# Weight bits in a PSUM bank, four heads through one bank in single pieces, and a new order of the opening and the first 16 steps

## The chip, the cores and the metric

The kernel runs on one core of one Trainium2 chip. The metric is the device time of one execution in microseconds (us). Engine names are those of the profile: PE does matmuls and transposes (PEld its weight loads), DVE, ACT and POOL are the vector, scalar and GpSimd engines, SP issues the DMAs. PE runs at one of two clocks, 2.4 or 1.2 GHz; the profile gives the granted clock as a share of the full one.

## The reference

Three parts in a row, for 4 batches of 576 tokens with 8 heads of 64 (2304 tokens of 512):

```python
scores = scale * np.matmul(q, k.transpose(0, 1, 3, 2))          # attention
mask_plain = (rel >= 0) & (rel < window)                        # heads 0-3, window 32
mask_dil = (rel >= 0) & (rel < window * dilation) & (rel % dilation == 0)   # heads 4-7, dilation 4
attn = softmax(np.where(mask, scores, -1e9)); x = attn @ v
...
h = x @ w_in                                                    # first MoE stage, d_ff 2048
g = h * np.cos(h)
x = g @ w_out
...
logits = x @ w_gate + noise_scale * noise                       # 8 experts, the best two of each token
out = sum over its two experts of weight * (relu(x @ w1[e]) @ w2[e])
```

## The kernel before

**Tiles and steps.** The tokens lie in 9 blocks of 256. The first MoE stage has 8 weight pairs p; one step is one block with one weight pair. The list `steps` has pairs p = 0 to 7, each for blocks 0 and 1 (16 steps), and then blocks 2 to 8 one after the other. Attention is cut into 16 "heads" u, each two heads of one batch; blocks 0 and 1 need heads 0 to 3, and heads 4 to 7 are worked beside steps 0 to 15. So the first 16 steps are also the time in which all weights arrive: each pair comes as four pieces of 512 columns.

**A weight piece.** `w_load` (L270) loads 512 KB of 64-bit numbers. `w_bits` makes 32-bit floats of their bits in three DVE operations on 128x512 elements (L291, L292, L293); the result `cut` lies in SBUF, and so do both inputs of L292 and L293. `w_parts` splits `cut` in a high part on ACT (L299) and a low part on POOL (L300). 4 pieces are cut in the opening, 28 beside steps 0 to 15.

**A head.** Scores in two halves of 5 and 4 blocks (mask matmul L422, product L431), the row maximum on DVE (L444, L446), nine Exp on ACT (L461, with a table load if another function was last), norm (POOL L475), three groups of transposes (PE L486) with their eviction (L489 on ACT, L491 on DVE), two output halves `mo` (PE L506), and the copy of these to `xraw` (L514, L523; on ACT in the opening, on DVE for heads 4 to 7). `x_split` makes the two float parts of x (ACT L548, DVE or POOL L549).

**A step.** The loop runs g1 (24 matmuls, L563, into a bank `ph`); position -1; ACT L571 and DVE L572; the first half of g2 of the step two before (6 matmuls, L590); position 0; Sin and Square on ACT (L574, L575) and DVE L576; position 1; g on ACT and POOL (L579, L580); the second half of that g2; position 2. The table `BESIDE` says which pieces of weights and heads are issued at which step and position. The string `OPENING` does the same for the time ahead of step 0: Q and V load a head, W, B, P stand for `w_load`, `w_bits`, `w_parts`, S, E, N, T, A for scores, Exp, norm, transposes and output of a head, X for `x_split`, G for a chunk of g1; steps 0 and 1 have three of their four chunks there.

**What sets the order.** Each engine takes its instructions in the order of the program and waits for their inputs. SP issues all loads in that order too. PSUM has 8 banks: two named `mid` that transposes, scores and output halves of heads 4 to 7 take in turn, two `ph`, four `acc`.

Of the kernel before, what the change touches and what calls it, by code (L numbers as in the profile page):

```python
# [208 lines left out]
def kernel(ctx: ExitStack, tc: tile.TileContext, qT, kT, v, wm, we, wg, noise, out):  # L209
# [66 lines left out]

    CUT = {}
# [38 lines left out]
    warm = psum.tile([P, 512], F32, tag="mid", name="warm", bufs=2)  # L316
# [86 lines left out]
    SM = {}  # L403

    def a_scores(u):
# [5 lines left out]
        if u in (2, 3):  # L411
            o = 4096 - (u - 1) * NB * KW
            s = ahead[2][:, o:o + NB * KW].rearrange("p (i k) -> p i k", k=KW)
        else:
            s = apool.tile([P, NB, KW], F32, tag="s", name=f"s{u}", bufs=2)
        mx = small.tile([P, NB], F32, tag="mx", name=f"mx{u}", bufs=3)
        for g, (i0, i1) in enumerate(((0, 5), (5, NB))):
            n = i1 - i0
            sc = psum.tile([P, 512], F32, tag=tag, name=f"sc{u}_{g}", bufs=bufs)
# [31 lines left out]
        U[u][2] = s  # L451

    def a_exp(u):
        s = U[u][2]
        if u not in SC:
            nc.scalar.activation(s, s, AF.Exp, scale=0.125)
            return
        mx, *s3 = SC.pop(u)
        sm = small.tile([P, NB], F32, tag="sm", name=f"sm{u}", bufs=3)
        for i in range(NB):  # L460
            nc.scalar.activation(s[:, i, :], s3[i // 5][:, i % 5, :], AF.Exp, scale=0.125, bias=mx[:, i:i + 1],  # L461
                                 accum_out=sm[:, i:i + 1])
        SM[u] = sm

# [13 lines left out]
    def a_trans(u, c, scalar=True):  # L478
        s = U[u][2]
        if u < 4:  # L480
            at = ahat[:, 3 * (u % 3) + c]
        else:
            at = apool.tile([KW, 3, P], F32, tag="at", name=f"at{u}_{c}", bufs=2)
        mid = psum.tile([P, 512], F32, tag="mid", name=f"mt{u}_{c}", bufs=2)
        for j in range(3):
            nc.tensor.transpose(mid[:KW, j * P:(j + 1) * P], s[:, 3 * c + j, :], ident)  # L486
        m3 = mid[:KW, :3 * P].rearrange("p (j q) -> p j q", q=P)
        if scalar:
            nc.scalar.activation(at, m3, AF.Copy)  # L489
        else:  # L490
            nc.vector.tensor_copy(at, m3)  # L491
        U[u][3 + c] = at

    def a_av(u, g, scalar=False):
        b, hp = divmod(u, 4)
        half = S // 2
        tag, bufs = ("mid", 2) if u >= 4 else ("acc", 4)
        mid = psum.tile([P, 512], F32, tag=tag, name=f"mo{u}_{g}", bufs=bufs)
# [17 lines left out]
        else:  # L516
            m3 = mid[:, :half].rearrange("p (r j) -> p r j", r=2)
            done = 0
            while done < SJ:
# [4 lines left out]
                done += n  # L524

# [225 lines left out]
    for u in range(4, FUSED):  # L751
        at_step(START[u - 4] + 2, -1, a_norm, u)
        at_step(START[u - 4] + 3, 0 if u == 4 else -1, a_part, u, 0)
    pieces = [(0, 2), (0, 3)] + [(j, k) for j in range(1, NPAIR) for k in range(4) if (j, k) > (1, 1)]
    for n, (j, k) in enumerate(pieces):
        i = n // 2
        if n % 2:
            at_step(i, 2, w_bits, j, k)
            at_step(*((i, 2) if i - 1 in START else (i + 1, 0)), w_parts, j, k)
        else:  # L760
            at_step(i, 0, w_bits, j, k)
            at_step(i, 1, w_parts, j, k)
        if j == NPAIR - 1:
            at_step(i - 2, 2, w_piece, j, k)
    for u in range(4, 16):
        i = START[u - 4]
        if i > 0:
            at_step(i, 2, a_scores, u)
        if i > 0:
# [5 lines left out]
        at_step(i + 3, 2, a_part, u, 1)  # L775
        at_step(i + 4, 0, a_part, u, 2)
# [107 lines left out]
    def t_trans(e, t):  # L884
# [7 lines left out]
        mid = psum.tile([P, 512], F32, tag="mid", name=f"mgx{e}_{t}", bufs=2)  # L892
# [87 lines left out]

    known = {f.__name__ + "(" + ",".join(map(str, a)) + ")": (f, a) for fs in extras.values() for f, a in fs}
# [9 lines left out]
    for i, (blk, p) in enumerate(steps):  # L991
        if i == 48:
# [130 lines left out]
    with tc.If(over > CAP):  # L1123
        nt = nc.values_load(nti[0:1, 1:2], min_val=NTILE, max_val=NTILE + -(-(NT - CAP) // P))
        with tc.For_i(NTILE, nt, 1) as i:
            with tc.For_i(0, NE, 1) as e:
# [17 lines left out]
                mid = psum.tile([P, 512], F32, tag="mid", name="gm", bufs=2)  # L1144
# [62 lines left out]
```

## Time and profile before

| | |
|---|---|
| median of 3 runs | 1021.38 us (1019.44 to 1021.94) |
| the profiled execution | 1020.52 us, span 1018.8 us, mean granted clock 0.988 |
| PE busy over the span | 979.7 us, 96% |
| DVE, ACT, POOL busy | 551.1 (54%), 458.2 (45%), 358.4 us (35%) |

A busy engine runs an instruction; a matmul at the lower clock is busy for longer. The share over the whole span is a mean over stages. Up to about 40 us the opening runs, up to about 168 us the 16 steps beside which weights and heads 4 to 7 are worked, and after that the steps have all weights.

### The profile page before, as it was taken

What the parts mean: (1) busy time and instruction counts of PE and PEld (TensorE: products, weight loads), DVE (VectorE), ACT (ScalarE), POOL (GpSimd) and SP (SyncE); (2) the same over time, 40 slices, a digit from 0 to 9 for tenths busy, and PEclk for the clock granted to TensorE, in tenths of its full rate; (3) what the DMA queues carried; (4) which work ended last, traced back from release to release, by engine and by line L of the source; (5) the groups of instructions that cost most, each with busy time, mean ns of one, the idle gap of its engine ahead of it and who ended that gap; (6) DMA issues with size and microseconds to landing.
All of it is one profiled execution on the core that took longest, in us unless ns stands there. A gap on an engine that the chain in (4) does not pass through costs nothing.

```text
span 1018.8 us, 16807 instructions
## 1 busy us (share of the span) xinstructions
PE 979.7 (96%) x6560; PEld 864.1 (85%) x6560; DVE 551.1 (54%) x1149; ACT 458.2 (45%) x909; POOL 358.4 (35%) x470
## 2 busy tenths in 40 slices
PE   8788899999999899999999999999999999999996
PEld 6676778988898788898887889898898979898895
DVE  7799885357653755443556756344453535354321
ACT  6646665565655565454555434233241414232110
POOL 5555554233343442424243232231313232322302
PEclk9898999999999999999999999999999999999999
DMA  9963203134221220000052555453434244441201
GB/s 210 325 219 101 81 25 74 57 94 123 58 92 35 64 42 15 22 1 22 2 201 76 138 153 169 141 168 113 152 123 150 73 164 139 148 161 40 84 11 59
DMA packets 70594, 105.11 MB, mean 103 GB/s; under 512 B 31252, under 2 KB 44820, under 8 KB 70513
## 3 DMA queue, kind: packets, MB, share of 16 engines
q1 hardware_dynamic: 60528, 76.34, 24.8%
q0 software_dynamic: 9984, 27.68, 8.8%
q8 instruction: 52, 0.85, 0.4%
q14 instruction: 30, 0.24, 0.1%
HBM read 85.41 MB, written 19.59 MB: 103 GB/s over the span
## 4 chain that ended last, share of the span: by engine, by line
PE 69%; DVE 13%; ACT 6%; DMA 5%; issue 4%; POOL 1%; SPq 1%; ACTq 0%; POOLq 0%; DVEq 0%
PE ye L947 20%; PE pe L912 20%; PE ph L563 12%; PE acc L590 11%; DVE cut L292 3%; DMA raw<-in_wm 2%; PE mgx L895 2%; DVE r L572 1%; DVE cut L291 1%; PE sc L431 1%; DVE cut L293 1%; DVE r L576 1%; ACT r L574 1%; ACT r L575 1%; PE mo L506 1%
## 5 line engine op out<-in xcount | busy, mean ns | idle before, releaser
L563 PE MATMUL ph<-xhl,wm 128*128 128x256 f32 x1728 | 229.7, 289 | 10.4 <-ACT wm L299 4.3
L563 PEld LDWEIGHTS ph<-xhl,wm 128*128 128x128 f32 x1728 | 219.4, 195 | 18.4 <-ACT wm L299 4.7
L947 PE MATMUL ye<-we,h 128*128 128x512 f32 (+1 forms) x960 | 229.5, 395 | 0.0
L590 PE MATMUL acc<-wm,g 128*128 128x512 f32 x864 | 220.5, 399 | 3.1 <-POOL g L580 1.2
L947 PEld LDWEIGHTS ye<-we,h 128*128 128x128 f32 (+1 forms) x960 | 172.9, 183 | 42.9
L590 PEld LDWEIGHTS acc<-wm,g 128*128 128x128 f32 x864 | 156.9, 190 | 34.4 <-POOL g L580 2.1
L580 POOL TENSOR_TENSOR g<-r,g 128x512 fp32r<-128x512 f32 x72 | 95.7, 1330 | 206.9 <-ACT g L579 206.3
L912 PE MATMUL pe<-xga,we 128*128 128x352 f32 x768 | 125.5, 324 | 0.0
L912 PEld LDWEIGHTS pe<-xga,we 128*128 128x128 f32 x768 | 122.6, 188 | 0.4 <-issue 0.4
L960 POOL DMA_INDIRECT out<-old,tir x35 | 35.5, 1013 | 224.1 <-DVE old L958 219.3
L915 DVE SCALAR_TENSOR_TENSOR h<-pe,h 128x256 fp32r<-128x256 f32 (+1 forms) x128 | 60.5, 474 | 91.5 <-ACT h L914 86.0
L914 ACT ACTIVATE h<-pe 128x256 fp32r<-128x256 f32 (+1 forms) x128 | 54.3, 424 | 123.9 <-PE pe L912 112.6
L958 DVE SCALAR_TENSOR_TENSOR old<-ye,wts,old 128x512 f32<-128x512 f32 (+1 forms) x35 | 26.2, 750 | 135.6 <-PE ye L947 132.0
L912 PE MATMUL pe<-xgb,we 128*128 128x256 f32 x768 | 94.8, 284 | 1.5 <-DVE h L915 1.1
L912 PEld LDWEIGHTS pe<-xgb,we 128*128 128x128 f32 x768 | 93.3, 192 | 2.2 <-DVE h L915 1.3
L572 DVE SCALAR_TENSOR_TENSOR r<-r,ph 128x512 f32<-128x512 int32 x72 | 49.2, 683 | 82.2 <-ACT r L571 77.5
L576 DVE SCALAR_TENSOR_TENSOR r<-r,ph 128x512 f32<-128x512 f32 x72 | 49.4, 686 | 81.4 <-ACT r L575 81.3
L828 DVE TENSOR_TENSOR we<-wraw,we 128x512 fp32r<-128x512 f32 x128 | 88.9, 704 | 4.2 <-ACT g L579 0.9
L827 ACT ACTIVATE we<-wraw 128x512 fp32r<-128x512 f32 x128 | 78.0, 623 | 0.0
L574 ACT ACTIVATE r<-r 128x512 f32<-128x512 f32 x72 | 45.4, 631 | 63.8 <-DVE r L572 63.7
L571 ACT ACTIVATE r<-ph 128x512 int32<-128x512 f32 x72 | 42.6, 592 | 51.2 <-PE ph L563 51.0
L579 ACT ACTIVATE g<-r 128x512 fp32r<-128x512 f32 x72 | 45.4, 631 | 43.3 <-DVE r L576 27.7
(190 smaller groups left out, 1027.5 us busy)
## 6 DMA issues: line engine op xcount, KB each, us to landing
wraw<-in_we SPq DMA_DIRECT2D x64, 512.0 KB
raw<-in_wm SPq DMA_DIRECT2D x28, 512.0 KB
vts<-in_v SPq DMA_DIRECT2D x13, 384.0 KB
x1d<-x SPq DMA_DIRECT2D x9, 512.0 KB
out<-zt SPq DMA_DIRECT2D x18, 256.0 KB
kts<-in_kT SPq DMA_DIRECT2D x13, 288.0 KB
qts<-in_qT SPq DMA_DIRECT2D x26, 144.0 KB
piece<-in_wm SPq DMA_DIRECT2D x4, 512.0 KB
```

The source lines that it names most:

```text
L563: nc.tensor.matmul(ph[:, j, :], w[:, a, o:o + P], t[:, x, c, :], start=(c == 0 and n == 0 and (j == 0 or len(cs) == 4)), stop=(c == 3 and ...
L572: nc.vector.scalar_tensor_tensor(r, n, -TWO_PI, ph, op0=ALU.mult, op1=ALU.add)
L574: nc.scalar.activation(r, r, AF.Sin, scale=0.5)
L576: nc.vector.scalar_tensor_tensor(r, r, 0.5, ph, op0=ALU.subtract, op1=ALU.mult)
L580: nc.gpsimd.tensor_tensor(g[:, 1, :], r, g[:, 0, :].bitcast(F32), op=ALU.subtract)
L590: nc.tensor.matmul(ACC[blk][t], g[:, a, j * TB + t * P:j * TB + (t + 1) * P], w[:, x, 1024 + j * DM:1024 + (j + 1) * DM], start=(p == 0 an ...
L827: nc.scalar.activation(t[:, 0, fs], raw, AF.Copy)
L828: eng.tensor_tensor(t[:, 1, fs], raw, t[:, 0, fs].bitcast(F32), op=ALU.subtract)
L912: nc.tensor.matmul(ph[:, :n], w[:, a, o:o + P], x[:, b, c, :], start=(c == 0 and i == 0), stop=(c == 3 and i == 2))
L914: nc.scalar.activation(h[:, 0, f, :], ph[:, :n], AF.Relu)
L915: nc.vector.scalar_tensor_tensor(h[:, 1, f, :], ph[:, :n], 0.0, h[:, 0, f, :].bitcast(F32), op0=ALU.max, op1=ALU.subtract)
L947: nc.tensor.matmul(acc, h[:, a, f, o:o + n], w[:, b, (f % 4) * DM:(f % 4 + 1) * DM], start=(f == 0 and i == 0), stop=(f == 7 and i == 2))
```

## The change

**Bits.** In steps 0 to 15 (the list `alone` is not empty there) the first two DVE operations of `w_bits` write a PSUM bank (tag `cut`, one bank), and the third reads it and the raw piece and writes `cut` in SBUF. L309 and L310, as they are called now, have one input in SBUF instead of two. In the opening the bits stay in SBUF.

**Banks.** The bank comes from `mid`: there is one bank `mid` and one `cut` (`mid_tile`). In steps 0 to 15 all transposes, scores and outputs of heads 4 to 7 take the one bank `mid`; from step 16 on both are taken in turn as before.

**Pieces.** Heads 4 to 7 come in single pieces: `a_s` and `a_e` for half of the scores and of the Exp, `a_tr` for a third of the transposes, `a_o` for half of the output with its `xraw` copy on ACT (L546) and not on DVE. `w_parts` comes as `w_hi` (ACT, L319) and `w_lo` (POOL, L324). For heads 6 and 7 the Sin of a step stands between the two halves of Exp, so that ACT has four more table loads.

**Order.** `OPENING` and the rows of `BESIDE` for steps 0 to 15 are new.

```diff
 OPENING = (
-    "S0 S1 E0 N0 Q4 E1 W01 S2 W02 T00 T01 N1 E2 S3 T02 T10a N2 A00 T11 A01 W10 E3 W11 T12 T20a A10a T21a "
...
-    "B10 G10 W23 G11 W12 W21 E4 B11 A30a A31a X30 P10 P11 X31p G01 G02 G12 W13 W22"
+    "W01 S0 S1 E0 N0 E1 S2 N1 E2 T00 T01 S3 T10a E3 N2 W10 T11 T02 N3 A00 A10a A01 T20a T12 B00 T21a A11a "
+    "T30a Q4 W20 X01 X11p B01 A20a T32a T22a X00p X10 S4 P00 A21a W02 X21p G00 X20p V4 B10 G01 W13 G10 "
+    "G11 W03 P01 W11 E4 T31a A30a A31a W22 W12 W23 W21 B11 G12 X30 P10 P11 G02 X31p"
 )
 BESIDE = """
...
-4:1 w_parts(3,0) w_load(4,3) a_scores(5)
...
+4:1 a_loadv(5) w_hi(3,0) w_lo(3,0) a_s(5,0) w_bits(3,1) w_bits(3,2) a_e(5,0) w_hi(3,2)
+4:2 a_s(5,1) w_load(4,1)
...
+    def mid_tile(name):
+        turn[0] += not alone
+        return psum.tile([P, 512], F32, tag="mid" if alone or turn[0] % 2 else "cut", name=name, bufs=1)
...
-        V.tensor_scalar(t, hw, 3, 0x3FFFFFF8, op0=ALU.logical_shift_left, op1=ALU.bitwise_and)
-        V.scalar_tensor_tensor(t, hw, 0xC0000000, t, op0=ALU.bitwise_and, op1=ALU.bitwise_or)
-        V.scalar_tensor_tensor(t, lw, 29, t, op0=ALU.logical_shift_right, op1=ALU.bitwise_or)
+        b = psum.tile([P, 512], F32, tag="cut", name=f"bits{j}_{k}", bufs=1).bitcast(U32) if alone else t
+        V.tensor_scalar(b, hw, 3, 0x3FFFFFF8, op0=ALU.logical_shift_left, op1=ALU.bitwise_and)
+        V.scalar_tensor_tensor(b, hw, 0xC0000000, b, op0=ALU.bitwise_and, op1=ALU.bitwise_or)
+        V.scalar_tensor_tensor(t, lw, 29, b, op0=ALU.logical_shift_right, op1=ALU.bitwise_or)
...
-        tag, bufs = ("mid", 2) if u > 4 else ("ph", 2) if u == 2 else ("acc", 4)
...
+            if u > 4:
+                sc = mid_tile(f"sc{u}_{g}")
...
+    def a_o(u, g):
+        a_av(u, g, True)
...
+        if i == 0:
+            alone.append(True)
+        if i == 16:
+            alone.clear()
```

The order on ACT late in the opening, before (`mt3_1` and `mo3_0`, `mo3_1` are a transpose and the outputs of head 3, `sc4` the scores of head 4; the last row is the first operation of step 0):

```order
L299 ACTIVATE wm0_435<-cut0_1_466 128x512
L489 ACTIVATE ahat_89<-mt3_1_526 96x384
L461 ACTIVATE s4_504,sm4_559<-sc4_0_506,mx4_505 128x96 x5
L461 ACTIVATE s4_504,sm4_559<-sc4_1_516,mx4_505 128x96 x4
L523 COPY xraw_82<-mo3_0_573 128x2x144
L523 COPY xraw_82<-mo3_1_585 128x2x144
L548 ACTIVATE xhl0_448<-xraw_82 128x256
L299 ACTIVATE wm1_538<-cut1_0_539 128x512
L299 ACTIVATE wm1_538<-cut1_1_569 128x512
L548 ACTIVATE xhl1_445<-xraw_82 128x256
L571 ACTIVATE r0_0_633<-ph0_0_531 128x512
```

And in the changed kernel:

```order
L555 COPY xraw_82<-mo2_1_503 128x2x144
L592 ACTIVATE xhl1_445<-xraw_82 128x256
L592 ACTIVATE xhl0_476<-xraw_82 128x256
L319 ACTIVATE wm0_413<-cut0_1_450 128x512
L494 ACTIVATE s4_481,sm4_558<-sc4_0_483,mx4_482 128x96 x5
L494 ACTIVATE s4_481,sm4_558<-sc4_1_493,mx4_482 128x96 x4
L521 ACTIVATE ahat_89<-mt3_1_568 96x384
L555 COPY xraw_82<-mo3_0_573 128x2x144
L555 COPY xraw_82<-mo3_1_585 128x2x144
```

The eviction of head 3's transpose stands now behind the nine Exp of head 4, not ahead of them.

The order of SP's loads ahead of step 0, from head 4's load (`kts`, `qts`) on, before:

```order
L248 DMA kts_83<-in_kT 128x576
L251 DMA qts_85<-in_qT 64x9x64 x2
L270 DMA raw0_104<-in_wm 128x1024 x2
L270 DMA raw1_378<-in_wm 128x1024 x2
L270 DMA raw0_104<-in_wm 128x1024
```

And in the changed kernel:

```order
L277 DMA raw0_104<-in_wm 128x1024
L277 DMA raw1_350<-in_wm 128x1024
L255 DMA kts_83<-in_kT 128x576
L258 DMA qts_85<-in_qT 64x9x64 x2
L277 DMA raw2_443<-in_wm 128x1024
```

Two weight pieces of 512 KB have moved ahead of head 4's load.

The order on PE in steps 2 and 3, where head 4 (`mt4`, `mo4`) is transposed, before:

```order
L563 MATMUL ph0_1_692<-xhl0_448,wm1_538 128x256 x24
L590 MATMUL acc0_0_720<-wm0_435,g0_0_649 128x512 x6
L486 MATMUL mt4_0_729<-ident_131,s4_504 96x128 x3
L486 MATMUL mt4_1_735<-ident_131,s4_504 96x128 x3
L590 MATMUL acc0_1_721<-wm0_435,g0_0_649 128x512 x6
L506 MATMUL mo4_0_773<-at4_0_728,vts_84 64x64 x6
...
L486 MATMUL mt4_2_787<-ident_131,s4_504 96x128 x3
L563 MATMUL ph1_1_792<-xhl1_445,wm1_538 128x256 x24
```

And in the changed kernel:

```order
L607 MATMUL ph0_1_695<-xhl0_476,wm1_529 128x256 x24
L634 MATMUL acc0_0_726<-wm0_413,g0_0_656 128x512 x6
L518 MATMUL mt4_0_735<-ident_131,s4_481 96x128 x3
L518 MATMUL mt4_1_742<-ident_131,s4_481 96x128 x3
L538 MATMUL mo4_0_747<-at4_0_734,vts_84 64x64 x6
...
L518 MATMUL mt4_2_772<-ident_131,s4_481 96x128 x3
L634 MATMUL acc0_1_727<-wm0_413,g0_0_656 128x512 x6
L607 MATMUL ph1_1_797<-xhl1_445,wm1_529 128x256 x24
```

The second half of g2, which stood between transposes and output, stands now behind all four of them, which follow one another in one bank.

The order on ACT at step 8, where head 6 has its Exp, before:

```order
L461 ACT_TABLE_LOAD
L461 ACTIVATE s6_1231,sm6_1262<-sc6_0_1233,mx6_1232 128x96 x5
L461 ACTIVATE s6_1231,sm6_1262<-sc6_1_1242,mx6_1232 128x96 x4
L299 ACTIVATE wm5_1226<-cut5_1_1256 128x512
L579 ACTIVATE g0_4_1285<-r0_4_1213 128x512
```

And in the changed kernel:

```order
L494 ACT_TABLE_LOAD
L494 ACTIVATE s6_1238,sm6_1249<-sc6_0_1240,mx6_1239 128x96 x5
L319 ACTIVATE wm4_1076<-cut4_3_1212 128x512
L618 ACT_TABLE_LOAD
L618 ACTIVATE r0_4_1229<-r0_4_1229 128x512
L619 ACTIVATE r0_4_1229<-r0_4_1229 128x512
L319 ACTIVATE wm5_1256<-cut5_0_1257 128x512
L494 ACT_TABLE_LOAD
L494 ACTIVATE s6_1238,sm6_1249<-sc6_1_1263,mx6_1239 128x96 x4
```

The halves of head 6's Exp stand apart, with a Sin between them. On PE the two halves of its scores (`sc6_0`, `sc6_1`) still follow one another with nothing between them, in one bank where there were two.

## Rows read from the trace of the kernel before

**Rows 1.** Busy time by window: start:end, length, PE, PEld, DVE, ACT, POOL, clock, DMA.

```profile
40.00:168.00 128.00, 110.47 (x774) 94.90 (x774) 111.70 (x150) 76.61 (x165) 72.97 (x58) 0.93 0.42 129
168.00:300.00 132.00, 129.89 (x1006) 115.67 (x1007) 75.33 (x211) 75.84 (x118) 47.60 (x56) 1.00 0.24 72
```

**Rows 2.** The chain in order of time: start, length, engine, work.

```profile
53.59 1.66 DVE cut L292
```

**Rows 3.** DVE busy time in that stage for L291, L292, L293 in turn.

```profile
40.00:168.00 128.00, 17.94 (x28) 0.93 0.42 129
40.00:168.00 128.00, 34.36 (x28) 0.93 0.42 129
40.00:168.00 128.00, 29.46 (x28) 0.93 0.42 129
```

**Rows 4.** Timeline: start, length, engine, line; one piece's L291 and L293, another's L292.

```profile
34.51 0.43 DVE L291 TENSOR_SCALAR cut<-raw 128x512 uint32<-128x512 uint32 x1
...
35.70 0.69 DVE L293 SCALAR_TENSOR_TENSOR cut<-raw,cut 128x512 uint32<-128x512 uint32 x1
...
44.82 1.66 DVE L292 SCALAR_TENSOR_TENSOR cut<-raw,cut 128x512 uint32<-128x512 uint32 x1
```

**Rows 5.** The page's costliest groups: busy us, mean ns, idle before.

```profile
L572 DVE SCALAR_TENSOR_TENSOR r<-r,ph 128x512 f32<-128x512 int32 x72 | 49.2, 683 | 82.2 <-ACT r L571 77.5
```

**Rows 6.** Timeline of DVE in the opening: a copy out of PSUM.

```profile
20.75 0.55 DVE L491 COPY ahat<-mt 96x384 f32<-96x384 f32 x1
```

**Rows 7.** The page's DMA rate in 40 slices of 25.5 us.

```profile
GB/s 210 325 219 101 81 25 74 57 94 123 58 92 35 64 42 15 22 1 22 2 201 76 138 153 169 141 168 113 152 123 150 73 164 139 148 161 40 84 11 59
```

**Rows 8.** Timeline, end of the opening; brackets: idle before and releaser.

```profile
28.98 2.25 PE L431 MATMUL sc<-kts,qts 128*128 128x96 f32 x10 [1.83 <-DMA qts<-in_qT]
...
33.33 0.49 ACT L489 ACTIVATE ahat<-mt 96x384 f32<-96x384 f32 x1 [0.79 <-PE mt L486]
...
34.02 0.34 ACT L461 ACTIVATE s<-sc,mx 128x96 f32<-128x96 f32 x1 [0.21 <-DVE mx L446]
...
35.38 1.39 PE L506 MATMUL mo<-ahat,ahead 96*64 96x64 f32 x40
...
36.88 1.27 ACT L523 COPY xraw<-mo 128x288 f32<-128x288 f32 x2
...
40.01 0.60 ACT L571 ACTIVATE r<-ph 128x512 int32<-128x512 f32 x1
```

**Rows 9.** Timeline of ACT and PE in steps 2 and 3.

```profile
54.26 0.85 ACT L489 ACTIVATE at<-mt 96x384 f32<-96x384 f32 x2
...
54.79 0.80 PE L506 MATMUL mo<-at,vts 96*64 96x64 f32 x20 [0.73 <-ACT at L489]
...
55.81 3.12 PE L563 MATMUL ph<-xhl,wm 128*128 128x256 f32 x24
```

**Rows 10.** PE's waits, 0 to 168: total us, times, longest us.

```profile
PE ph L563 <- ACT wm L299: 4.3, 2, 3.3
PE ph L563 <- POOL wm L300: 2.7, 5, 0.9
PE mo L506 <- ACT at L489: 2.5, 2, 1.7
PE mt L486 <- POOL s L475: 2.3, 4, 0.9
...
PE sc L422 <- DVE xraw L523: 1.2, 1, 1.2
```

**Rows 11.** Timeline at step 8: head 6's maximum and table load.

```profile
112.69 0.65 DVE L444 TENSOR_REDUCE mx<-sc 128x5 f32<-128x480 f32 x1
...
113.62 1.28 ACT L461 ACT_TABLE_LOAD   x1 [0.19 <-DVE mx L446]
```

**Rows 12.** Timeline of PE: first g2 with the last weight pair.

```profile
170.94 2.91 PE L590 MATMUL acc<-wm,g 128*128 128x512 f32 x12
```

More of the change, by code (lines that the diff above doesn't have):

```diff
@@ L102 @@
-15:-1 w_parts(7,3) x_split(2,2,3,1)
+0:-1 w_bits(0,2) a_loadqk(5)
+0:0 w_load(3,0)
+0:1 w_bits(0,3) w_hi(0,2) w_lo(0,2)
+0:2 w_hi(0,3) w_lo(0,3) a_norm(4)
+1:-1 w_load(4,0)
+1:0 w_bits(1,2)
+1:1 w_hi(1,2) w_bits(1,3) w_lo(1,2)
+2:-1 w_load(4,2) w_load(3,3) w_load(3,2)
+2:0 a_tr(4,0) w_hi(1,3) a_tr(4,1) a_o(4,0) w_lo(1,3) w_bits(2,0)
+2:1 w_hi(2,0) a_tr(4,2) w_bits(2,1) w_lo(2,0)
+2:2 w_bits(2,2)
+3:0 w_hi(2,1) w_lo(2,1)
+3:1 w_hi(2,2) w_load(3,1)
+4:-1 w_bits(2,3) w_lo(2,2)
+4:0 w_load(5,0) w_hi(2,3) a_o(4,1) w_lo(2,3) w_bits(3,0)
@@ L103 @@
+11:1 w_bits(7,0) w_hi(6,3) w_lo(6,3)
+11:2 a_e(7,1) a_norm(7)
+12:0 w_hi(7,0) w_lo(7,0) w_bits(7,1)
+12:1 w_hi(7,1) w_lo(7,1)
+12:2 w_piece(7,2) w_piece(7,3)
+13:0 a_tr(7,0)
+13:1 w_bits(7,2)
+14:-1 a_loadv(7)
+14:0 a_tr(7,1) w_bits(7,3) a_loadqk(8)
+14:1 a_o(7,0) a_tr(7,2) w_hi(7,2)
+14:2 a_o(7,1) x_split(2,0,2) w_lo(7,2)
+15:-1 x_split(2,2,3,1) w_hi(7,3) w_lo(7,3)
 15:0 x_split(2,3,4,1)
@@ L275, in w_piece @@
         RAW[j, k] = t
+    turn = [0]
+    alone = []
+    def mid_tile(name):
+        turn[0] += not alone
+        return psum.tile([P, 512], F32, tag="mid" if alone or turn[0] % 2 else "cut", name=name, bufs=1)
     CUT = {}
@@ L403, with a_scores @@
     SM = {}
-    def a_scores(u):
+    MX = {}
+    def a_scores(u, gs=(0, 1)):
         hp = u % 4
         fused = u < FUSED
-        tag, bufs = ("mid", 2) if u > 4 else ("ph", 2) if u == 2 else ("acc", 4)
         q_, k_ = U[u][:2]
         m = masks[hp // 2]
[L411 to L417, printed above, removed]
-            n = i1 - i0
-            sc = psum.tile([P, 512], F32, tag=tag, name=f"sc{u}_{g}", bufs=bufs)
+        if 0 in gs:
+            if u in (2, 3):
+                o = 4096 - (u - 1) * NB * KW
+                s = ahead[2][:, o:o + NB * KW].rearrange("p (i k) -> p i k", k=KW)
+            else:
+                s = apool.tile([P, NB, KW], F32, tag="s", name=f"s{u}", bufs=2)
+            U[u][2] = s
+            MX[u] = small.tile([P, NB], F32, tag="mx", name=f"mx{u}", bufs=3)
+        s, mx = U[u][2], MX[u]
+        for g in gs:
+            i0, i1 = ((0, 5), (5, NB))[g]
+            n = i1 - i0
+            if u > 4:
+                sc = mid_tile(f"sc{u}_{g}")
+            else:
+                tag, bufs = ("ph", 2) if u == 2 else ("acc", 4)
+                sc = psum.tile([P, 512], F32, tag=tag, name=f"sc{u}_{g}", bufs=bufs)
             if fused:
@@ L450, in a_scores, with a_exp @@
                                     op=ALU.subtract)
-        U[u][2] = s
-    def a_exp(u):
+    def a_exp(u, gs=(0, 1)):
         s = U[u][2]
-        if u not in SC:
+        if u >= FUSED:
             nc.scalar.activation(s, s, AF.Exp, scale=0.125)
             return
[L458 to L463, printed above, removed]
+        if 0 in gs:
+            SM[u] = small.tile([P, NB], F32, tag="sm", name=f"sm{u}", bufs=3)
+        for g in gs:
+            s3 = SC.pop((u, g))
+            for i in range(5 * g, (5, NB)[g]):
+                nc.scalar.activation(s[:, i, :], s3[:, i - 5 * g, :], AF.Exp, scale=0.125, bias=MX[u][:, i:i + 1],
+                                     accum_out=SM[u][:, i:i + 1])
     def a_norm(u):
@@ L774 @@
             at_step(i + 3, 0, a_part, u, 0)
[L775 to L776 removed]
+            at_step(i + 3, 2, a_part, u, 1)
+            at_step(i + 4, 0, a_part, u, 2)
         if u + 1 < 16:
@@ L979 @@
     at_step(71, 2, split_we, 0, 2, 0)
+    for u in range(4, FUSED):
+        for n in range(2):
+            if u > 4:
+                at_step(0, 0, a_s, u, n)
+                at_step(0, 0, a_e, u, n)
+            at_step(0, 0, a_o, u, n)
+        for c in range(3):
+            at_step(0, 0, a_tr, u, c)
+    for j in range(NPAIR):
+        for k in range(4):
+            if (j, k) not in ((0, 0), (0, 1), (1, 0), (1, 1)):
+                at_step(0, 0, w_hi, j, k)
+                at_step(0, 0, w_lo, j, k)
     known = {f.__name__ + "(" + ",".join(map(str, a)) + ")": (f, a) for fs in extras.values() for f, a in fs}
```

99 lines of the change are left out of this document (43 added, 56 removed), and 1 row of the table OPENING.

## The prediction

> **What bounds the kernel now.** I read the busy time by window first, and of it the ratio of PE to DVE. From 168 us on PE works 129.9 of 132 us at full clock; nothing else counts there, and a shift of the end of the stage before it goes straight to the end of the kernel. In the stage from 40 to 168 us PE works only 110.5 of 128 us, DVE 111.7, ACT 76.6, and the granted clock is 0.93 [rows 1]. So the stage holds 17.5 us of idle PE, and some of its busy time is at the lower of the two clocks. The chain of what ended last runs in this stretch through the weight bits on DVE, in pieces such as L292 at 53.6 us [rows 2]. The wait list says the same from PE's side: g1 waits for ACT's and POOL's halves of a weight piece for 4.3 and 2.7 us, which wait for DVE's bits themselves; 1.2 us are a wait for an `xraw` copy on DVE; 2.5 and 2.3 us belong to head 4 to 7's own chain (eviction, norm) [rows 10]. The opening, up to 40 us, is bounded by loads and by ACT's order: head 4's scores wait for their load [rows 8].
>
> **The bits.** 28 pieces cost 17.94 + 34.36 + 29.46 = 81.8 us of DVE, 2.92 each [rows 3]. A piece at its fastest costs 0.43 + 0.69 + 0.69 = 1.81 [rows 4]; L292 also takes 1.66, and the mean of L292 is 34.36/28 = 1.23. L572, the same kind of operation with one input in PSUM and the other in SBUF, takes 0.683 on the mean of 72, so it hardly ever is slow [rows 5]. After the change L309 and L310 have one SBUF input, as L572 has: 0.69 each. No row shows DVE writing PSUM with this operation. Bounds: 0.69 from L572, and 1.66 from the slow L292, were the write to cost what the second input cost. I take 0.69, since L572 is the nearest in form.
>
> L308 reads SBUF and writes PSUM. A copy out of PSUM of 384 columns takes 0.55, that is 0.73 for 512 [rows 6]; its bounds are 0.43 (as L291) and 0.73, and I take 0.68. A piece is then 0.68 + 0.69 + 0.69 = 2.06, and 28 pieces save 28 x 0.86 = 24 us of DVE. With some 4 us of `xraw` copies moved to ACT, DVE falls to about 84 of 128 us and stops being the engine that sets the stage.
>
> The Trainium skill, "VectorE: DVE Perf Modes", section "Why PSUM operands drop a tier", says that an operand in PSUM takes the fast mode from a DVE operation, fp32 falling to the plain rate; this speaks against the change, since of the three operations the first now runs fast from SBUF. By the row of the fast L291 alone a piece would be 1.81 and the saving 31 us; by that rule it is the 24 us above. No row here shows the bits in PSUM; the slower PSUM copy agrees with the rule. Seven us of DVE are not what decides, so both leave the sum below as it is.
>
> **What of it reaches PE.** Not 24 us: PE can only get back its idle time. The waits with DVE at their root are 4.3 + 2.7 + 1.2 = 8.2 us. The most that can go is 17.5 less the 2.5 and 2.3 of the heads' own chain, 12.7 [rows 1, 10]. Middle: **-10.4**. The clock of 0.93 means up to 0.07 x 110.5 = 7.7 us of slow matmuls, which fell where PE had been idle. Part of the idle places go and new ones come (below), so I take half: **-3.9**, bounds -7.7 and 0.
>
> **The opening.** `Q4` now goes out behind W01 and W10. At 325 GB/s, the rate of the second slice, 512 KB take 1.6 us [rows 7]; two pieces are 3.2 us, and the scores of head 4 waited for that load already (1.83 us, start 28.98). I take +2.9, so 31.9, and the first Exp of head 4, 34.02 before, starts at 36.9 if ACT is free. ACT has four short operations ahead of it (a copy and its conversions, half a microsecond each by the 0.49 of the eviction and 1.27 for two copies), one of which waits for an output that PE now makes behind these scores: up to +1.3. The nine Exp take 36.88 - 34.02 = 2.86. Only behind them comes the eviction of head 3's transpose, which was at 33.33, ahead of them: 39.8 to 41.1, and 0.5 more to its end. Then the two outputs of head 3 (1.39 on PE, with handoffs 1.6), then their copies: 41.9 to 43.2 against 36.88. All that follows on ACT (conversion, two high parts, conversion, L571 of step 0) keeps its order, so L571's successor comes 5.0 to 6.3 late, at 45.0 to 46.3 for 40.01 [rows 8]. I take **+5.7**. The lower bound is +2.1: Q4 lands as before, and only the place behind the Exp counts (34.02 + 2.86 + 0.5 + 1.6 = 39.0). Before, the Exp of head 4 lay beside PE's output of head 3; that cover is gone.
>
> **Steps 2 and 3.** Head 4's two transposes had two banks and the two evictions came as a pair in 0.85, with the second half of g2 on PE in between. Now transpose, eviction, transpose, eviction, output, copy and third transpose follow one another in one bank with no g2 between. PE waits for three emptyings (0.43 each and about 0.3 of handoff), less the 0.73 that it waited already and the copy's overlap: (3 x 0.73) less 0.73 is 1.5, and ACT has step 1's g and step 2's L615 in its queue, half a microsecond more: **+2.1**, bounds 0 (PE would wait for the weights of step 3 anyway) and 2.5 [rows 9]. With the opening this puts step 3's g1 at 63.6 for 55.81.
>
> **Scores in one bank.** Heads 6 and 7 issue both halves on PE with nothing between. The second half waits until the first is read by the last of its five Exp: from the maximum's start to the table load 113.62 - 112.69 = 0.93, table load 1.28, five Exp at 2.86/9 each 1.6: 3.8 us of idle PE for each head [rows 8, 11]. Head 5 has half a g2 between its halves (2.91/2), so 2.4 [rows 12]. Sum **+10.0**; behind the waiting matmul stand the second half of g2 and the next g1. Bounds: 11.4 if head 5 pays in full, and 3 if most of it lies where PE would have waited for weights at the next step anyway. The same bank serves transposes and outputs of heads 5 to 7, but these stand in positions apart, with g1 or g2 between, and I cost them at nothing; without that cover it would be 0.5 for each of the 15. The four extra table loads (5.1 us) and the copies bring ACT to about 86 of 128, which leaves room; at head 6 and 7 they are in the 3.8.
>
> **Sum.** 5.7 + 2.1 + 10.0 - 10.4 - 3.9 = +3.5. The profiled execution is 1020.52, so 1024.0; the median is 0.9 above it, so 1024.9, and I say 1025. A change of 0.3%, about 3.1 us, is what a measurement of this kernel can tell from none.
>
> **Rivals.**
> - *The waits on the one bank fall into idle time, and the relief shows in full.* Weights are still cut at nearly the same steps, so a PE that waits 3.8 us at head 6 gives DVE, ACT and POOL time to get ahead, and the next g1 doesn't wait. Then the scores cost 3 for 10.0 and relief is 12.7: 5.7 + 2.1 + 3 - 12.7 - 3.9 = -5.8, 1015.6. For it: both sides come from the same 17.5 us. It decides as soon as less than 3.4 of the 10.0 reach the end. Against it: PE's order is fixed, and L572 to L576 of a step wait behind the same PE. Chance 0.25.
> - *The opening's delay is mostly absorbed.* +2.1 for 5.7, since the weights of steps 1 and 2 arrive no later than before: 0 in all, 1021. Chance 0.20.
> - *The bits get no cheaper* (a write to PSUM costs what the second SBUF input did, or the slow L292 has another cause). Then DVE stays at its 111 us, the relief is gone but for the 1.2 of the copies and the clock stays: 5.7 + 2.1 + 3 to 10 - 1.2 = +10 to +17, 1031 to 1038. Against it: the 72 executions of L572. Chance 0.10.
> - *The forecast*, +1 to +7, 1022 to 1028: 0.45.
>
> **How the numbers follow.** Faster by over 0.3%: the first rival but for a small part, 0.22. Within: the second (0.20), a quarter of the forecast's range (0.11) and the edge of the first, 0.34. Slower: three quarters of the forecast (0.34) and the third, 0.44. The range goes from 1015 to 1030; it leaves out the third rival and the low edge of the first. The forecast's own is 1022 to 1028.
>
> **What would show it.** In the changed kernel: L309 and L310 close to 0.69 with hardly any at 1.66, L308 near 0.68, some 58 us for the 28 pieces. First L615 at 45 to 46. PE idle ahead of `sc5_1`, `sc6_1`, `sc7_1`, released by ACT's Exp, 2.4 to 3.8 each. Almost no wait of g1 for L319 or L324. The g2 that started at 170.94 [rows 12] starts near 174.5, and all behind it is shifted by as much. It is wrong if that g2 starts before 170 (first rival), or if L309's mean stays over 1.1 (third); a first L615 before 43 would move it to the second.

## The result

The changed kernel takes 1028.21 us in the median of 5 runs (1026.84 to 1029.22) and the kernel before 1021.38 in the same series: a ratio of 1.0066 with a 95% interval of 1.0045 to 1.0087, some 6.8 us more. The forecast was 1025, slower, in a range of 1015 to 1030.

The windows of the changed kernel, with the same columns as [rows 1] and the same stretches:

```profile
40.00:168.00 128.00, 105.42 (x754) 92.92 (x750) 85.91 (x138) 85.64 (x188) 62.59 (x56) 0.89 0.40 128
168.00:300.00 132.00, 130.18 (x1018) 115.80 (x1019) 73.65 (x201) 75.31 (x119) 46.06 (x51) 1.00 0.25 75
```

DVE is relieved as meant, 85.9 us for 111.7. PE, which should have gained by it, works 105.4 for 110.5 us of the stage, and its granted clock has fallen from 0.93 to 0.89. From 168 us on both kernels are alike. All of the loss is made before. The time lies in the range and just past the upper end of the forecast's own 1022 to 1028.

What PE waits for in the changed kernel up to 176 us (total us, times, longest), to be laid beside [rows 10]:

```profile
PE sc L454 <- ACT s L494: 8.4, 2, 4.4
PE sc L459 <- ACT s L494: 3.3, 1, 3.3
PE mt L518 <- ACT at L521: 3.0, 1, 3.0
PE mo L538 <- DMA ahead<-in_v: 2.7, 2, 1.5
PE ph L607 <- POOL xhl L593: 2.0, 1, 2.0
```

The waits of g1 for weight pieces (4.3 and 2.7 us before) are gone. In their place stand waits for the one bank: second halves of scores (L454, L459) for the Exp that reads the first half, 11.7 us, and head 4's second transpose for the eviction of the first, 3.0.

The timeline of PE shows them in place (start, length, engine, line; idle before and releaser in brackets):

```profile
57.84 0.84 PE L518 MATMUL mt<-ident,s 128*96 128x128 f32 x3 [3.01 <-ACT at L521]
59.39 1.28 PE L538 MATMUL mo<-at,vts 96*64 96x64 f32 x20 [0.71 <-ACT at L521]
...
64.37 3.04 PE L607 MATMUL ph<-xhl,wm 128*128 128x256 f32 x24
...
81.84 0.48 PE L459 MATMUL sc<-mask,identb 128*128 128x384 bf16 x1 [3.33 <-ACT s L494]
82.12 1.86 PE L463 MATMUL sc<-kts,qts 128*128 128x96 f32 x8
83.68 5.07 PE L607 MATMUL ph<-xhl,wm 128*128 128x256 f32 x24
...
115.24 0.32 PE L454 MATMUL sc<-mask,identb 128*128 128x384 bf16 x1 [4.04 <-ACT s L494]
...
144.58 0.48 PE L454 MATMUL sc<-mask,identb 128*128 128x384 bf16 x1 [4.36 <-ACT s L494]
...
179.19 1.09 PE L634 MATMUL acc<-wm,g 128*128 128x512 f32 x4
```

Behind such a wait PE runs slowly: the g1 at 83.68 takes 5.07 us, the one at 64.37 3.04. The windows of PE alone (length, busy, granted clock, DMA) behind the four waits show it at or near the lower clock:

```profile
56.00:64.00 8.00, 4.85 (x31) 0.59 0.23 92
84.00:88.00 4.00, 4.00 (x20) 0.50 0.65 166
116.00:120.00 4.00, 4.00 (x19) 0.64 0.42 107
144.00:148.00 4.00, 3.42 (x13) 0.50 0.00 0
```

The last row of the timeline is the g2 that started at 170.94 before [rows 12], 8.25 us later; the span is 7.7 longer.

### The profile page after: what moved, and what is told of

It is laid out like the page before. It is cut to its first block, busy times and chain, and to the rows that moved or that the text cites. A ratio compares the mean times of both kernels' runs of the same rounds, so it can differ in the third digit from the quotient of the medians.

```text
span 1026.5 us, 16823 instructions
## 1 busy us (share of the span) xinstructions
PE 984.1 (96%) x6560; PEld 870.1 (85%) x6560; DVE 524.8 (51%) x1135; ACT 468.2 (46%) x927; POOL 351.4 (34%) x470
## 4 chain that ended last, share of the span: by engine, by line
PE 81%; DVE 6%; ACT 5%; DMA 3%; POOL 1%; issue 1%; SPq 1%; ACTq 0%; POOLq 0%; DVEq 0%
PE pe L952 21%; PE ye L987 20%; PE ph L607 17%; PE acc L634 15%; PE sc L463 2%; PE mgx L935 2%; PE mo L538 1%; PE mt L518 1%; DMA raw<-in_wm 1%; ACT r L619 1%; ACT r L618 1%; PE mx L661 1%; DMA qts<-in_qT 1%; DMA ahead<-in_qT 1%; DVE r L620 1%
## 5 line engine op out<-in xcount | busy, mean ns | idle before, releaser
L607 PE MATMUL ph<-xhl,wm 128*128 128x256 f32 x1728 | 225.6, 288 | 2.5 <-POOL xhl L593 2.0
L624 POOL TENSOR_TENSOR g<-r,g 128x512 fp32r<-128x512 f32 x72 | 92.9, 1290 | 226.2 <-ACT g L623 226.1
L620 DVE SCALAR_TENSOR_TENSOR r<-r,ph 128x512 f32<-128x512 f32 x72 | 49.5, 687 | 85.9 <-ACT r L619 85.8
L615 ACT ACTIVATE r<-ph 128x512 int32<-128x512 f32 x72 | 42.7, 594 | 63.3 <-PE ph L607 60.6
```

What stands on the lines that cost most here:

```text
L607: nc.tensor.matmul(ph[:, j, :], w[:, a, o:o + P], t[:, x, c, :], start=(c == 0 and n == 0 and (j == 0 or len(cs) == 4)), stop=(c == 3 and ...
L620: nc.vector.scalar_tensor_tensor(r, r, 0.5, ph, op0=ALU.subtract, op1=ALU.mult)
L624: nc.gpsimd.tensor_tensor(g[:, 1, :], r, g[:, 0, :].bitcast(F32), op=ALU.subtract)
```

## The experiments

Each ratio is against the kernel before, measured on the same chip in the same series. A difference between two of them is given in us at 0.1% to 1.02 us; by the intervals of the two, it is uncertain by some 2 to 3 us either way.

| kernel | ratio, 95% interval |
|---|---|
| the changed kernel | 1.0066 (1.0045 to 1.0087) |
| with the old opening | 1.0011 (0.9996 to 1.0026) |
| second halves in the other bank | 1.0054 (1.0033 to 1.0075) |
| bits in SBUF, one bank | 1.0149 (1.0124 to 1.0174) |
| bits in SBUF, two banks | 1.0102 (1.0082 to 1.0121) |
| kernel before with the new opening | 1.0040 (1.0022 to 1.0057) |
| head 4's load first | 1.0046 (1.0032 to 1.0060) |
| second halves in the other bank, head 6 spaced | 0.9990 (0.9972 to 1.0008) |
| that, old opening, head 4 spaced | 0.9915 (0.9896 to 0.9934) |
| that, no bits behind Exp | 0.9960 (0.9945 to 0.9975) |
| old order of work, new order of loads | 1.0083 (1.0066 to 1.0100) |
| 0.9915 with bits in SBUF | 1.0083 (1.0066 to 1.0100) |
| PE kept busy in the opening | 1.0086 (1.0063 to 1.0109) |

Two theories stood at the start: that PE's waits for the one bank make the loss (bank theory), and that the late start of step 0 is carried to the end (opening theory).

### The old opening in the changed kernel

```diff
-OPENING = ("W01 S0 S1 E0 N0 E1 S2 N1 E2 T00 T01 S3 ...
+OPENING = ("S0 S1 E0 N0 Q4 E1 W01 S2 W02 T00 T01 N1 ...    (the whole string of before)
```

> The changed kernel with the OPENING string of the kernel before; the table for the first 16 steps stays as changed. Opening theory (the first L615 at 45.5 us for 40.0 is carried through to the end): first L615 near 40, and the time falls by 4 to 6 us, from 1028.2 to 1022 to 1024. Bank theory (PE's waits for the one bank in steps 2 to 12 set the end, and a late start is absorbed in them): first L615 near 40 as well, but the time falls by no more than 2 us, to 1026 or above.

1.0011, 5.6 us less than the changed kernel. Its ACT timeline has step 0's first operation 3.4 us earlier than the changed kernel's 45.52, though at 40.01 before [rows 8], and the last-pair g2 starts at 175.29 for 179.19:

```profile
42.12 0.60 ACT L615 ACTIVATE r<-ph 128x512 int32<-128x512 f32 x1
```

What the opening loses is carried through. The bank waits are all still there (8.4 and 3.3 us). In both profiled executions PE's clock is at 0.50 from 24 to 32 us, so these 3.4 us are hardly the clock's.

### The second halves in the other bank

```diff
-                sc = mid_tile(f"sc{u}_{g}")
+                if alone and g:
+                    held.append(u)      # until this half's Exp is issued, w_bits keeps its bits in SBUF
+                sc = mid_tile(f"sc{u}_{g}", "cut" if alone and g else None)
...
-8:0 a_s(6,0) a_e(6,0) w_hi(4,3) w_bits(5,0) w_lo(4,3) a_s(6,1)
+8:0 a_s(6,0) a_s(6,1) a_e(6,0) w_hi(4,3) w_bits(5,0) w_lo(4,3)
```

> The changed kernel with the second half of the scores of heads 5, 6 and 7 in the bank of the weight bits, issued right behind the first half; the bits of the five pieces that are cut while that half waits for its Exp stay in SBUF. Bank theory: PE's waits for Exp ahead of the second halves (3.3 + 4.0 + 4.4 = 11.7 us) go, with the slow matmuls behind them; PE falls back on other waits for a part; the first g2 with the last weight pair starts at 169 to 173 us for 179.2, the time is 1018 to 1022. Opening theory: the waits go but g1 waits for weights in their place, and the time stays at 1026 to 1028.

1.0054, inside the changed kernel's interval: the waits are gone and the time is not. PE's timeline says why:

```profile
127.16 0.87 PE L526 MATMUL mt<-ident,s 128*96 128x128 f32 x3 [8.43 <-POOL s L515]
```

Head 6's transposes stand right behind step 9's g1 in the new table. With PE ahead of its old pace they come before the Exp and the norm of that head are done, and the saved time is waited off there. A part of the wait is the edit's own: ahead of the norm, DVE had a piece of bits that waited for the lent bank until the last Exp had read it:

```profile
123.81 0.69 DVE L312 TENSOR_SCALAR bits<-raw 128x512 uint32<-128x512 uint32 x1 [2.54 <-ACT s L500]
```

By itself this run would have spoken against the bank theory; the wait it names was the next thing to move.

### That, with head 6 spaced

```diff
-8:0 a_s(6,0) a_s(6,1) a_e(6,0) w_hi(4,3) ...
-8:1 w_hi(5,0) a_e(6,1) ...
+8:0 a_s(6,0) a_s(6,1) w_hi(4,3) ...
+8:1 w_hi(5,0) a_e(6,0) a_e(6,1) ...
-9:-1 a_tr(6,0)
-9:1 a_tr(6,1) w_hi(5,2) w_lo(5,1)
+9:1 a_tr(6,0) w_hi(5,2) w_lo(5,1)
+9:2 a_tr(6,1) w_bits(5,3)
```

> As the run with the second halves in the other bank, but the two halves of Exp of heads 6 and 7 come together behind the step's Sin (two table loads fewer each), and head 6's first two transposes stand behind the first half of g2 of step 9 and at its end, not right behind its g1. Bank theory (the waits ahead of the second halves cost PE 11.7 us; in the earlier run an 8.4 us wait of head 6's transposes for its norm only took their place): no wait over 2 us in steps 5 to 13, and the time is 5 to 8 us below the changed kernel, at or just under the kernel before. Rival (the waits are covered, and g1 will wait for weights): the time stays within 2 us of the changed kernel.

0.9990, 7.8 us less than the changed kernel, at the upper end of what the bank theory gave. The edit also saves the four table loads that the change had added and moves head 6's transposes, so the 7.8 us are not the bank's alone. "No wait over 2 us" was missed; one of 5.4 is left ahead of head 6's transposes (the 3.0 is head 4's, in step 2, as before):

```profile
PE mt L525 <- ACT g L630: 5.4, 1, 5.4
PE mt L525 <- ACT at L528: 3.0, 1, 3.0
```

### That, with the old opening and head 4 spaced

```diff
-2:0 a_tr(4,0) w_hi(1,3) a_tr(4,1) a_o(4,0) w_lo(1,3) w_bits(2,0)
+2:0 a_tr(4,0) a_tr(4,1) w_hi(1,3) w_lo(1,3) w_bits(2,0)      # a_tr(4,1) in the bank of the bits
+2:2 a_o(4,0) w_bits(2,2)
+3:0 a_tr(4,2) w_hi(2,1) ...
```

> As the run with head 6 spaced, with the OPENING of the kernel before as well, and with head 4's second transpose in the bank of the bits, its output and third transpose behind g2 halves as before. If the three costs add up (opening 5.6, second halves 5 to 8, head 4's wait of 3.0): 8 to 12 us below the changed kernel, 0.2 to 0.5% faster than the kernel before. If they hide one another: at the time of the kernel before, within 0.1%.

0.9915: 15.4 us below the changed kernel and the fastest of all. The sum was expected at 8 to 12. If the parts add up, 5.6 for the opening and 7.8 for the second halves leave 2.0 for head 4, which was not run alone; that they do add up is not shown. In this profiled execution PE also stayed at full clock all through the opening, from 22 to 36 us, where those of the two runs it is put together from did not. The window from 48 to 176 us, of the changed kernel, of this one and of the kernel before:

```profile
48.00:176.00 128.00, 109.14 (x765) 96.23 (x765) 84.49 (x134) 83.79 (x183) 63.15 (x55) 0.90 0.35 110
```

```profile
48.00:176.00 128.00, 114.77 (x847) 100.94 (x846) 82.74 (x133) 83.57 (x186) 64.36 (x56) 0.97 0.35 109
```

```profile
48.00:176.00 128.00, 112.18 (x793) 96.14 (x792) 107.65 (x148) 76.51 (x166) 68.98 (x55) 0.95 0.36 105
```

The other engines did the same work as in the changed kernel. PE did more of its own (847 matmul records for 765), at 0.97 of its clock for 0.90. The clock is not all of it: in the run with head 6 spaced, 7.8 us below the changed kernel, it is 0.91 in this window.

### No bits behind the Exp

```diff
-8:1 w_hi(5,0) a_e(6,0) a_e(6,1) w_bits(5,1) w_hi(5,1) w_lo(5,0) a_norm(6)
+8:1 w_hi(5,0) w_bits(5,1) a_e(6,0) a_e(6,1) a_norm(6) w_hi(5,1) w_lo(5,0)
-11:1 a_e(7,0) a_e(7,1) w_bits(7,0) ...
+11:1 w_bits(7,0) a_e(7,0) a_e(7,1) ...
```

> As the run with the opening of before and all banks spaced (0.9915 of the kernel before), and besides: the bits of the two pieces that stood behind the Exp of heads 6 and 7 go ahead of it and stay in SBUF (there DVE waited 4.4 us for the bank and head 6's norm came behind the piece), and so do the bits of piece 3 of pair 1 (head 4's second transpose waited 2.3 us for them). If PE still pays for waits of that kind: the 5.4 and 2.3 us fall to 2 or less, and 3 to 6 us less than that run, 0.986 to 0.989 of the kernel before. If the next limit is right behind: within 2 us of that run, 0.990 to 0.993.

The 5.4 us fell to 3.2 and the 2.3 to 0.9, but the ratio is 0.9960, above the 0.9915 that it should have undercut. This profiled execution had ten us of half clock in the opening, which the other's had not, and the two were measured on different chips; whether the edit itself cost anything was not separated from that. The clock alone hardly explains it: three executions of the run of 0.9915 with mean clocks of 0.984 to 0.989 took 1015.8 to 1016.2 us, the four of this one at 0.986 and 0.987 took 1017.5 to 1021.1.

### Bits in SBUF, with one bank and with two

```diff
-        b = psum.tile(...).bitcast(U32) if alone else t
+        b = t
```

> The changed kernel with the weight bits in SBUF as before; the bank that held them is left unused, all else as changed. If the relief of DVE reaches PE as the prediction's sum had it (10.4 us of waits): DVE's three operations come back to 2.7 to 2.9 us a piece, g1 waits for weights again, 1034 to 1039. If it is hidden behind PE's waits for the one bank: pieces as dear, but the time is within 2 us of the changed kernel's, 1026 to 1030.

1.0149, 8.5 us above the changed kernel: the relief reaches PE, whatever else the change costs. (In the profiled execution up to 1.9 of this lie in the opening, which the edit leaves alone: first L615 at 47.44 for 45.52.) The lines view of DVE has the two operations with two SBUF inputs dear again:

```profile
L309 DVE SCALAR_TENSOR_TENSOR cut<-raw,cut 128x512 uint32<-128x512 uint32 x24 | 25.4, 1059 | 0.8
L310 DVE SCALAR_TENSOR_TENSOR cut<-raw,cut 128x512 uint32<-128x512 uint32 x24 | 25.0, 1042 | 0.8
```

g1 hardly waits for weights here, though it was expected to; the slower DVE shows elsewhere. The waits for Exp ahead of the second halves are 9.4 and 4.8 us for 8.4 and 3.3, the outputs of heads wait 4.0 us for evictions for 1.3, and the first g2 waits 2.3 us for its weights.

> The changed kernel with the weight bits in SBUF and both banks for the tiles of heads 4 to 7 in turn, as before the change; opening and table as changed. Against the run with the bits in SBUF and one bank it prices the second bank alone. Bank theory: PE's waits ahead of the second halves go, 6 to 10 us less than with one bank, and about the time of the kernel before or a few us above it, 1022 to 1027. Opening theory: within 2 us of the run with one bank.

1.0102, with `mid_tile` taking both banks in turn besides: 4.8 us less than with one, below the 6 to 10 expected. The waits for Exp go, and 9.8 us of waits of transposes for the norm take their place, as in the second run.

### The bits where the banks don't wait

The run of 0.9915 with the same edit, all bits in SBUF:

> As the run with the opening of before and all banks spaced (0.9915), but with all weight bits in SBUF. It prices the bits where PE's waits for the banks are gone. If waits for banks and waits for weights hid one another, the bits are worth more here than the 8.5 us that they were worth in the changed kernel: 12 us or more, 1.004 or above. If they add up: 7 to 10 us, 0.998 to 1.001.

1.0083: here the bits are worth 17 us, twice the 8.5. A part of the 17 may be the opening's clock, at half from 24 to 34 us in this run's profile and full in the other's (step 0 starts at 42.57 for 41.19), and the two were measured on different chips. Against the run with no bits behind Exp, which was measured beside it and had the half clock too, the bits are worth 12.5 us; that run differs from the one of 0.9915 by three pieces. Both are above 8.5: in the changed kernel part of DVE's relief was hidden behind PE's waits for the bank.

### What makes the opening dear

The new `OPENING` in the kernel before, and nothing else:

> The kernel before with the new OPENING string and nothing else of the change. Opening theory: the new order of the opening costs by itself what undoing it gave back, 4 to 6 us, whatever the steps behind it do; first L571 at 43 to 46 us and the time 0.4 to 0.6% above the kernel before. Rival (the late start counts only together with the one bank, since the old steps are bound by DVE and absorb it): first L571 as late, but the time within 0.2% of the kernel before.

1.0040: 4.1 us by itself, where undoing it gave 5.6; the two agree within their intervals. The first L571 came later than expected, at 47.65, behind a piece for which DVE waited:

```profile
44.41 0.50 DVE L291 TENSOR_SCALAR cut<-raw 128x512 uint32<-128x512 uint32 x1 [6.47 <-DMA raw<-in_wm]
```

That is W11, which the new order loads behind W20, W02, head 4's V, W13 and W03; the float parts of x that the next g1 chunk needs queue behind it on DVE.

The changed kernel with Q4 and W01 at their old places, all else in the new order:

```diff
-    "W01 S0 S1 E0 N0 E1 S2 ... T30a Q4 W20 ...
+    "S0 S1 E0 N0 Q4 E1 W01 S2 ... T30a W20 ...
```

> The changed kernel with Q4 and W01 at the places that they had before (Q4 behind N0, W01 behind E1); the order of all engines but SP stays as changed. If the loads make the opening late (W01 in flight beside the V loads lets PE wait for them twice, 1.3 and 1.5 us, after which its granted clock is 0.50 for ten us): those waits shrink to the 1.0 of before, head 4's scores start near 29.5 for 32.9, first L615 at 41 to 43 for 45.5, and 2 to 4 us less than the changed kernel. If ACT's order makes it late (the nine Exp ahead of head 3's eviction): first L615 stays at 44 to 46 and the time within 1 us of the changed kernel.

1.0046, 2.0 us less than the changed kernel, with intervals that overlap, so that no gain is not excluded. The detail expected failed: the waits for V did not shrink (3.1 us), the half clock lasted from 22 to 36 us, head 4's scores started at 33.38 and the first L615 at 46.59. These scores did not wait for their load any more; PE, at half clock, came to them late.

The changed kernel with the loads in the new order and the work of the four engines in the old one:

```diff
+    "W01 S0 S1 E0 N0 E1 S2 T00 T01 N1 E2 S3 T02 T10a ... E3 W10 T12 ... T30a Q4 W20 P00 ... W03 W11 E4 B11 ...
```

> The changed kernel with the opening's loads in the new order, and its work on PE, ACT, DVE and POOL in the old order. If the new order of the work makes the opening dear (PE comes to outputs of heads whose V is not there, with nothing else to do, and runs at half its clock after that): about as with the whole old opening, 1.000 to 1.002 of the kernel before. If the new order of the loads does: as the changed kernel, 1.005 to 1.008.

1.0083: nothing of the 5.6 us comes back. The new order of the loads is enough to make the opening dear, and the old order of the work does not help it. Whether the new order of the work is dear with all loads in the old order was not run. Scores wait for their load 3.7 us here, 2.8 of them head 4's first.

The last run filled the place where PE waits for V, ahead of A10a:

```diff
+        for n in range(12):
+            nc.tensor.matmul(fill_, flat[:, :P], flat, start=True, stop=True)
```

> The changed kernel with twelve matmuls on constants, whose result nothing reads, on PE ahead of head 1's first output (A10a), where PE waits twice for V. Clock theory (the new opening is dear because PE idles there and then runs ten us at a granted clock of 0.50): those waits are filled, the clock stays at 1.00 from 22 to 33 us, head 4's scores start at 28.5 to 30.5 for 32.9, first L615 at 42 to 44 for 45.5, and the time falls to 1.002 to 1.004 of the kernel before (1.0066). Load theory (the late loads set the end of the opening, and the clock only fills time that PE would have waited): the clock stays up all the same, but head 4's scores wait for their load or step 0 for its weights, first L615 stays above 44.5, and the time is within 0.1% of the changed kernel's.

1.0086, 2.0 us above the changed kernel (the load theory had it within 0.1%), with intervals that overlap: no gain. The clock did what both theories said, and the scores waited for their load, as only the load theory had it:

```profile
19.26 2.79 PE L783 MATMUL fill<-const-bfloat16-1.0 128*128 128x512 bf16 x12
...
22.48 0.66 PE L538 MATMUL mo<-ahat,ahead 96*64 96x64 f32 x16 [0.15 <-DMA ahead<-in_v]
...
33.41 2.42 PE L463 MATMUL sc<-kts,qts 128*128 128x96 f32 x10 [5.14 <-DMA qts<-in_qT]
```

The wait for V shrank from 2.7 to 0.2 us and the clock stayed at 1.00 to 32 us; PE was at head 4's scores by 28 and then waited 5.1 us for their load, which came when it had come before. In the changed kernel these scores wait 0.3 us, since the slow PE arrives late: the half clock there only fills time in which the load was not yet in. It did not go away, though. Behind the 5.1 us of waiting the clock is 0.50 from 34 to 40 us, where the changed kernel's is 1.00, and the first L615 comes at 48.49 for 45.52. So the two limits cover each other: with the load early and the clock low the scores started at 33.38, with the clock up and the load late at 33.41. In the new order of the work, both at once were not tried.

## Why the prediction came out as it did

**The bits** were sized right. A piece takes 0.69 + 0.70 + 0.69 = 2.07 us (2.06 forecast), from the lines view of DVE, 48 to 176 us:

```profile
L309 DVE SCALAR_TENSOR_TENSOR bits<-raw,bits 128x512 uint32<-128x512 uint32 x23 | 16.0, 696 | 0.8
L308 DVE TENSOR_SCALAR bits<-raw 128x512 uint32<-128x512 uint32 x23 | 15.8, 687 | 0.1
L310 DVE SCALAR_TENSOR_TENSOR cut<-raw,bits 128x512 uint32<-128x512 uint32 x23 | 15.8, 687 | 2.4
```

Writing PSUM costs what L572 paid, the row chosen [rows 5]; durations like the 1.66 of [rows 4] are gone. L308 takes 0.69, where L291 took 0.43 at its fastest [rows 4], which agrees with the Trainium skill, "VectorE: DVE Perf Modes", section "Why PSUM operands drop a tier". The stage lost little by it, since the mean of L291 there was 17.94/28 = 0.64 already [rows 3]: the prediction's "now runs fast from SBUF" held for 19 of the 28 executions, and the others took 0.51 to 1.53.

That L309 and L310 no longer come at 1.66 agrees with the Trainium skill, "SBUF — State Buffer", section "Who interferes with whom", by which a DVE instruction with two SBUF inputs contends with a GpSimd instruction that reads SBUF and one with at most one does not, outside the modes that use both ports: means of 1059 and 1042 ns with two SBUF inputs, 696 and 687 with one. The traces say the same one by one. In the kernel before, from 40 to 176 us, all 31 executions of L292 and L293 that took over 1 us ran beside POOL for at least half of their time, and the 20 with next to no POOL work beside them took 0.69. The L292 at 44.82 [rows 4] ran beside the first row here; in the changed kernel an L309 lies wholly beside such a row and takes 0.70, and none took longer:

```profile
44.59 1.34 POOL L300 TENSOR_TENSOR wm<-cut,wm 128x512 fp32r<-128x512 f32 x1 [2.02 <-ACT wm L299]
```

```profile
59.04 1.28 POOL L324 TENSOR_TENSOR wm<-cut,wm 128x512 fp32r<-128x512 f32 x1 [0.22 <-ACT wm L319]
59.53 0.70 DVE L309 SCALAR_TENSOR_TENSOR bits<-raw,bits 128x512 uint32<-128x512 uint32 x1
```

**What of it reaches PE**: 10.4 us forecast, 8.5 measured by the run with the bits in SBUF. The named waits of g1 went, as forecast.

**The opening**: +5.7 forecast; the first L615 came at 45.52, in the middle of the 45.0 to 46.3, and undoing it was worth 5.6 us. ACT's rows follow the steps of the working, from the Exp on:

```profile
38.17 0.32 ACT L494 ACTIVATE s<-sc,mx 128x96 f32<-128x96 f32 x1
...
41.01 0.49 ACT L521 ACTIVATE ahat<-mt 96x384 f32<-96x384 f32 x1
...
42.03 1.30 ACT L555 COPY xraw<-mo 128x288 f32<-128x288 f32 x2 [0.53 <-PE mo L538]
...
45.52 0.60 ACT L615 ACTIVATE r<-ph 128x512 int32<-128x512 f32 x1 [0.32 <-PE ph L607]
```

That the new order of the loads is enough for the loss is shown by the run with the old work. The prediction had only Q4 in mind, and there the number came out right partly by luck: head 4's scores started at 32.91 for the 31.9 assumed, but PE, at half clock, reached them hardly sooner than the load did, and putting Q4 and W01 back gave 2.0 us, not clear of none. How the loss divides between W11, which holds DVE, the V loads and the clock was not settled.

**Steps 2 and 3**: the g1 of step 3 was forecast at 63.6 and came at 64.37, 8.6 us later than before, of which 5.5 are the opening's. That leaves 3.0 for these steps, above the 2.1 and its upper bound of 2.5. Of the waits of head 4 (3.0, 0.7, 0.6) the first is the long one. In front of the eviction ACT had more than the half microsecond assumed: a high part that waited for DVE, g and L615. PE ran at 0.59 of its clock there.

```profile
55.60 0.63 ACT L319 ACTIVATE wm<-cut 128x512 fp32r<-128x512 f32 x1 [0.83 <-DVE cut L310]
...
57.22 0.47 ACT L521 ACTIVATE at<-mt 96x384 f32<-96x384 f32 x1
```

**The scores in one bank**: 10.0 us forecast, 11.7 of waits in the trace. Heads 6 and 7 cost 4.04 and 4.36 for 3.8, head 5 3.33 for 2.4, since its Exp waited 1.47 us for a maximum that DVE had behind other work:

```profile
78.78 1.28 ACT L494 ACT_TABLE_LOAD   x1 [1.47 <-DVE mx L478]
```

Taking the waits away was worth 7.8 us, once what they covered (head 6's norm) was moved too and with the four table loads saved.

**The term that failed is the clock**: -3.9 us, taken as half of what the slow matmuls of [rows 1] held. The bank waits make new idle places, and behind each of them PE is at the lower clock for a while, so the mean fell to 0.89 where it was to rise. Scores, relief and clock act for the most part between step 3's g1 and the first g2 with the last weight pair. There the forecast was 10.0 - 10.4 - 3.9, 4.3 us gained; measured, the delay goes from 8.56 to 8.25, 0.3 gained. The 4 us that are missing are the size of the clock term, but the trace does not divide them among the three.

Without this term the sum is 5.7 + 2.1 + 10.0 - 10.4 = +7.4, and 6.8 was measured. That it comes so near is partly luck. By the prediction's own working a clock of 0.89 means 0.11 x 105.4 = 11.6 us of slow matmuls for 7.7, a term of +3.9; and the prices that the runs gave, with the clock in them, are 7.8 for the scores and 8.5 for the relief, not 10.0 and 10.4. In the run of 0.9915, with the waits gone, the stage ran at 0.97 from 48 to 176 us; but those of 0.9990 and 0.9960 ran at 0.91 and 0.92 there, so the clock is not the whole price of the waits.

**The rivals.** The first (waits that fall into idle time) has this much for it, that the two sides overlap: the bits are worth 8.5 us with the waits and 12 to 17 without, the second bank 4.8 us with the dear bits, and the waits 7.8 with the cheap ones. But both of its prices fell: the scores cost 7.8 and not 3, and the relief gave 8.5 and not 12.7. The second (an opening mostly absorbed, +2.1) is against the 5.6 and 4.1 us of the opening's two runs, the third (bits no cheaper) against the 2.07 us of a piece.

## What to carry to other kernels

A buffer taken from an engine that waits in order must be paid back in the order of the work: DVE's 24 us were there, but two halves that followed each other in one bank cost PE as much as it gained, and lending the same bank to the second half, with the bits in SBUF for just that time and the order behind it moved, made most of both gains stand. When a wait is removed and the time stays, look for the next wait on the same chain (here the norm) before giving up the theory. An engine's late arrival can hide a late load: keep it busy, and the load shows. Two limits that end at the same time must be lifted together before either can be priced.

## What the runs showed that was not expected

The opening's clock is not the same in every execution. With the old opening PE waited for V near 22 us for 1.0 us in all in the profiled execution of the kernel before, 1.2 in the run of 0.9915, 1.3 in that of 0.9960 and 2.3 in the changed kernel with the old opening. The clock stayed at 1.00 to 28 and 40 us in the first two and was at 0.50 from 24 to 32 in the others. Executions of one kernel on one chip differ in their mean clock and their time together: with head 6 spaced, those with a mean clock of 0.986 and 0.987 took 1021.5 and 1020.2 us, those with 0.978 1025.4 and 1027.5. That the opening makes this difference is not shown, since only one execution of each kernel has a trace.
